# mLSTM and four experts on one core: w2's low halves made apart from chunk 4's scans, two outputs in two parts

## Chip, core and metric

The kernel runs on one core of one Trainium2 chip. The metric is device time in microseconds (us), lower is better. Times of the runs are medians; views of the profile come from one profiled execution.

## What is computed

An mLSTM layer (2 batches, 8 heads, 768 steps, head width 40) feeds a mixture of 4 experts (model width 320, hidden width 1024). All arrays are float32.

```python
# mLSTM, per time step t
m_new = max(f[t] + m, i[t])
C = exp(f[t] + m - m_new) * C + exp(i[t] - m_new) * outer(v[t], k[t])
n = exp(f[t] + m - m_new) * n + exp(i[t] - m_new) * k[t]
y[t] = sigmoid(o[t]) * (C @ q[t]) / max(|n . q[t]|, 1)
# experts on x = y, 1536 rows of 320
p = domain_probs / (domain_probs.sum(-1) + 1e-9)
out = sum over e of p[:, e] * (relu(x @ w1[e]) @ w2[e])
```

## The kernel before

The 1536 rows are cut into 12 chunks of 128 (`NCH`), 6 per batch. Every engine works through its instructions in the order in which the program issues them; nothing reorders them, so the order of the calls is the schedule. SyncE (SP) issues every transfer.

**A chunk n** needs: `decay(n)` (VectorE, two scans of 128x512 that build the decay matrix dd; for chunks 0 to 3 the factors fb come from TensorE and lie in PSUM, from chunk 4 on they come by a transfer of 512 KB, `load_f`, and lie in SBUF), `scores(n)` (TensorE), `weigh(n)` (VectorE, scores times dd), `values(n)` and `keys(n)` (GpSimd; `keys` needs dd), `inter(n)` (TensorE, then eight ScalarE copies into yb), `intra(n)` (TensorE), `norm(n)` (VectorE, six operations that end in xr), `state(n)` (TensorE, then two VectorE additions into the next state cs), `carry(n)` (GpSimd, the decayed state cd), `turn(n)` (three TensorE transposes of xr, then ScalarE copies into the high part of xst) and `turn_lo(n)` (VectorE, the low part).

**PSUM.** The results of `inter`, `intra`, `state` and `turn` (y1, y0, st, px) take turns in the pool `ps_y`, which has two buffers. So st takes the buffer of y1, px that of y0, and the next y1 and y0 those of st and px.

**The experts** use split numbers: each weight is a high part (float32r, made by a ScalarE copy, `split_hi`) and a low part (the difference, made by a subtraction, `split_lo`). `split_w2(f, 2)` does both for two of the eight hidden blocks f of w2; `quarter_hi(i)` and `quarter_lo(i)` do it for blocks 2i and 2i+1 of w1. Products are summed over three or more pairs of parts.

Expert 0 works on groups of 256 rows while the chunks go on. A group has four `hidden` steps (two blocks each: 16 matmuls on TensorE, relu on ScalarE for the high part of h, a VectorE operation for its low part) and two `output` steps (24 matmuls each: eight blocks times three pairs of h and w2 parts; then one ScalarE copy). For group 0 the list of an output is sorted so that the 16 matmuls with the high part of w2 come ahead of the 8 with its low part. `steps(k)` issues the next k steps; `SLOTS` says for each chunk how many stand after `decay`, after `carry`, and around `turn`. After chunk 11 come expert 0's last rows and experts 1 to 3, by 512 rows, on TensorE almost alone.

The raw w2 of expert 0 (`w2r`, 1,310,720 bytes) is requested at L603, behind `f_d` at L601. In the loop's turn n = 2, at L679 to L681, the four `split_w2` stand at its end, behind `carry(3)`. Turn n = 3 begins with `decay(4)` (L660), then `steps` with the hidden step of blocks 6 and 7 (L661).

Of the kernel before, what the change touches and what calls it, by code (L numbers as in the profile page):

```python
# [8 lines left out]
F32 = mybir.dt.float32  # L9
# [7 lines left out]
NE, DM, FF = 4, 320, 1024  # L17
NT = B * S
L = 128
# [6 lines left out]
NF = FF // L  # L26
HI, LO = 0, 1
# [9 lines left out]
NPE = 4  # L37

SLOTS = (
    (0, 1, 0), (1, 1, 1), (1, 1, 1), (1, 1, 0), (1, 1, 0),  # L40
    (1, 1, 0), (1, 1, 0), (1, 1, 0), (1, 1, 1), (0, 1, 1),
)
PAD = 56

# [5 lines left out]
def tile_mlstm_moe(ctx, tc, gt, qk, vk, ot, dp, w1, w2, out):  # L50
    ctx.enter_context(tc.manual_schedule())
    nc = tc.nc

    def pool(name, bufs, **kw):
        return ctx.enter_context(tc.tile_pool(name=name, bufs=bufs, **kw))
# [9 lines left out]
    ps_o = pool("ps_o", 2, space=PSUM)  # L65
# [22 lines left out]
    def new_weights(e):  # L88
        wp = wps[e % 2]
        w1s = wp.tile([L, KW, FF], F32R, tag="w1", name=f"w1s{e}")  # L90
        if e == 0:
            nc.gpsimd.memset(w1s[C:L, 5].bitcast(F32), 0.0)
        return w1s, wp.tile([L, 2, NF, DM], F32R, tag="w2", name=f"w2s{e}")

    def split_hi(hi, raw):
        nc.scalar.activation(hi, raw, AF.Copy)  # L96

    def split_lo(lo, hi, raw, eng):
        eng.tensor_sub(lo, raw, hi.bitcast(F32))  # L99
# [8 lines left out]
    def split_w2(ws, f0, n, raw, eng):  # L108
        f = slice(f0, f0 + n)
        split_hi(ws[:, HI, f], raw[:, f])  # L110
        split_lo(ws[:, LO, f], ws[:, HI, f], raw[:, f], eng)

    def load_w1e(e):
        raw1 = raws.tile([L, 3, FF], F32, tag="raw", name="raw1")
        nc.sync.dma_start(raw1, w1[e])
        return raw1
# [8 lines left out]
    class Expert:  # L125


        def __init__(self, e, t0, n, w1s, w2s):
            self.e, self.t0, self.n, self.w1s, self.w2s = e, t0, n, w1s, w2s
            self.nf, self.wide = W // n, n == W  # L130
            self.hs = []
            self.nh, self.no = NF // self.nf, n // L
            self.i = 0
            self.banks = []

        def step(self):
            i = self.i
            self.i += 1
            if i < self.nh:
                self.hidden(i * self.nf)  # L140
            elif i < self.nh + self.no:
                self.output(i - self.nh)
            return self.i < self.nh + self.no

        def hidden(self, f0):
            n, nf = self.n, self.nf
# [34 lines left out]
                    start=True, stop=False,  # L181
                )

        def output(self, t):
            e, ws = self.e, self.w2s
            po = ps_o.tile([L, DM], F32, tag="po", name="po")
            sl = slice(t * L, (t + 1) * L)
            ks = [(f, a, b) for f in range(NF) for a, b in ((HI, LO), (HI, HI), (LO, HI))]
            if e == 0 and self.t0 == 0:
                ks.sort(key=lambda k: k[2])  # L190
            for i, (f, a, b) in enumerate(ks):
                nc.tensor.matmul(  # L192
                    po, self.hs[f][a][:, sl], ws[:, b, f, :],
                    start=(i == 0), stop=(i == len(ks) - 1),
                )
            i = self.t0 // L + t
            if e == 0:
                nc.scalar.activation(acc[:, i, :], po, AF.Copy, scale=pw[:, i, 0:1])  # L198
            else:
                nc.vector.scalar_tensor_tensor(  # L200
                    out=acc[:, i, :], in0=po, scalar=pw[:, i, e:e + 1], in1=acc[:, i, :],
                    op0=ALU.mult, op1=ALU.add,
                )
            if e == NE - 1:
                nc.sync.dma_start(out[i * L:(i + 1) * L, :], acc[:, i, :])


    with ExitStack() as actx:
# [4 lines left out]
        w1s, w2s = new_weights(0)  # L213
        w1r = {}

        def quarter_hi(i):
            f, (ab, c) = slice(i * G, (i + 1) * G), w1r[i]
            split_hi(w1s[:, 0:2, f], ab)
            split_hi(w1s[:, 2, f], c)
# [138 lines left out]
        def load_qk(j, c=None):  # L358
            c = slice(0, 2) if c is None else slice(c, c + 1)
            nc.sync.dma_start(qks[j % 2][:, c], qk[j, :, c])  # L360

        def load_vk(j, c=None):
            if j not in vks:
                vks[j] = a2.tile([L, 2, 2, H, D], F32, tag="vk", name="vk")
            c = slice(0, 2) if c is None else slice(c, c + 1)
            nc.sync.dma_start(vks[j][:, c], vk[j, :, c])

        def load_o(j):
            nc.sync.dma_start(acc[:, 2 * j:2 * j + 2], ot[:, 2 * j:2 * j + 2])

        def gate_o(j):
            og = acc[:, 2 * j:2 * j + 2]
            nc.scalar.activation(og, og, AF.Sigmoid)
# [4 lines left out]
        def spread(n, pool, tag):  # L378

            b, c, k = n // NC, n % NC, 48 if n < 2 else L  # L380
            fbs[n] = [pool.tile([L, 4, L], F32, tag=tag, name="fb") for _ in range(2)]
            for h in range(H):
                nc.tensor.matmul(
                    fbs[n][h // 4][:, h % 4, :],
                    sel[0:k, b * H + h:b * H + h + 1].to_broadcast([k, L]),
                    fr[0:k, c * L:(c + 1) * L], start=True, stop=True,
                )

        def load_f(n):
            b, c = n // NC, n % NC  # L390
            fb = a0.tile([L, H, L], F32, tag=f"fb{n % 2}", name="fb")
            fbs[n] = fb[:, 0:4], fb[:, 4:8]
            nc.sync.dma_start(
                fb, f_d[b * H:(b + 1) * H, c * L:(c + 1) * L].unsqueeze(0).to_broadcast([L, H, L])
            )

        def decay(n):
            dds[n] = a1.tile([L, H, L], F32, tag=f"dd{n % 2}", name="dd")
            for i in range(2):
                nc.vector.tensor_tensor_scan(  # L400
                    out=dds[n][:, 4 * i:4 * i + 4].rearrange("p h t -> p (h t)"),
                    data0=fbs[n][i].rearrange("p h t -> p (h t)"),
                    data1=id4.rearrange("p h t -> p (h t)"),
                    initial=0.0, op0=ALU.mult, op1=ALU.add,
                )
# [8 lines left out]
        def keys(n):  # L414
            if n % NC < NC - 1:
                nc.gpsimd.tensor_mul(  # L416
                    kp[n % 2][:, :, 0:D], vks[n // 2][:, n % 2, 1],
                    dds[n][:, :, L - 1:L].to_broadcast([L, H, D]),
                )
# [37 lines left out]
        def carry(n):  # L457
            b, c = n // NC, n % NC
            if 0 < c < NC - 1:
                cd = cds[n] = a1.tile([104, NP, L], F32, tag="cd", name="cd")  # L460
                nc.gpsimd.tensor_mul(  # L461
                    cd, cs[c % 2][0:104],
                    bl[0:104, c, b * NP:(b + 1) * NP].unsqueeze(2).to_broadcast([104, NP, L]),
                )
# [63 lines left out]
        def steps(n):  # L528
            for _ in range(n):
                if not work[0].step():  # L530
                    work.pop(0)
# [70 lines left out]
        w2r = raws.tile([L, NF, DM], F32, tag="raw", name="w2r")  # L602
# [30 lines left out]
        gate_l(2, NC)  # L633
        spread(3, ps_o, "po")
        keys(2)
        carry(2)
        gctx.close()
        a0 = actx.enter_context(
# [4 lines left out]
        for n in range(2, NCH):  # L643
            j, cc = n // 2, n % 2
            k = SLOTS[n - 2]
            nxt = n + 1 < NCH
            if cc == 0 and j + 1 < NG:
                load_qk(j + 1)
                load_vk(j + 1)
            if NPE < n + 2 < NCH:  # L650
                load_f(n + 2)
            if cc == 0:
                if j > 1:
                    gate_o(j)
                if j + 1 < NG:
                    load_o(j + 1)
            if n == NCH - 2:
                raw1 = load_w1e(1)
            if nxt:
                decay(n + 1)  # L660
            steps(k[0])  # L661
            if n == 2:
                quarter_hi(2)
                quarter_lo(2)
            inter(n)
            intra(n)
            norm(n)
            if n == 2:
                quarter_hi(3)
                quarter_lo(3)  # L670
            if nxt:
                scores(n + 1)
            state(n)
            if nxt:
                values(n + 1)
                keys(n + 1)
                weigh(n + 1)
                carry(n + 1)
            if n == 2:  # L679
                for f in range(0, NF, 2):  # L680
                    split_w2(w2s, f, 2, w2r, nc.gpsimd)  # L681
            steps(k[1])
            if cc == 0:
                steps(k[2])
            turn(n)
            turn_lo(n)
            if cc == 1:
                steps(k[2])
# [112 lines left out]
```

## Time and profile before

| | us |
|---|---|
| median of 3 runs (411.93 to 412.13) | 411.93 |
| the profiled execution | 413.2 |
| span of its profile | 411.4 |
| TensorE busy in the span | 401.2 |
| VectorE, ScalarE, GpSimd busy | 181.6, 125.2, 85.2 |

In the rows further below, PE is TensorE (PEld its weight loads), DVE VectorE, ACT ScalarE, POOL GpSimd, SPq SyncE's queue of transfers. L192 is line 192: the matmuls of `output`; L157 those of `hidden`; L400 the scans; L96 and L99 the copies and subtractions that split weights. A number in brackets is time in which the engine sat idle before the row, with what ended it. PEclk is the granted clock of TensorE as a share of 2.4 GHz (0.50 is 1.2 GHz). Times count from the start of the span.

### The profile page before, as it was taken

How to read it: one execution, taken by the hardware profiler on the slowest of the kernel's cores; microseconds unless marked ns; L12 is line 12 of the kernel's file. 1: busy time of each engine (PE TensorE's matmuls, PEld its weight loads, DVE VectorE, ACT ScalarE, POOL GpSimd, SP SyncE). 2: the span in 40 equal slices, each digit the busy share in tenths (PEclk: the TensorE clock that was granted, in tenths of full speed). 3: DMA queues.
4: the chain of work that ended last, by engine and by line, in shares of the span. 5: the costliest groups of instructions: out<-in, count | busy, mean ns of one | idle time of the engine just before them, and what ended most of it. 6: DMA issues, size and time to landing. Idle time of an engine off the chain costs nothing.

```text
span 411.4 us, 7176 instructions
## 1 busy us (share of the span) xinstructions
PE 401.2 (98%) x3042; PEld 363.2 (88%) x3042; DVE 181.6 (44%) x319; ACT 125.2 (30%) x298; POOL 85.2 (21%) x98
## 2 busy tenths in 40 slices
PE   9899699999999999999999999999999999999996
PEld 5699599999988898998988988989989889899896
DVE  8989958697962303314214234133142251231321
ACT  5676133352433533205213032033030140220210
POOL 6869401223112630003410010016100010000000
PEclk9999699999999999999999999999999999999999
DMA  7997514576000213000300004002000000001001
GB/s 212 309 287 203 162 53 106 177 200 237 2 2 2 77 52 118 35 2 0 129 0 2 0 2 153 2 2 90 39 0 2 0 2 32 33 0 49 17 18 48
DMA packets 15080, 29.34 MB, mean 71 GB/s; under 512 B 1000, under 2 KB 10728, under 8 KB 13736
## 3 DMA queue, kind: packets, MB, share of 16 engines
q1 hardware_dynamic: 15048, 28.88, 22.8%
q8 instruction: 24, 0.39, 0.4%
q14 instruction: 8, 0.07, 0.1%
HBM read 26.86 MB, written 2.02 MB: 70 GB/s over the span
## 4 chain that ended last, share of the span: by engine, by line
PE 89%; DVE 8%; issue 2%; ACT 0%; DVEq 0%
PE po L192 41%; PE ph L157 37%; DVE dd L400 3%; PE ph L179 3%; PE s L427 2%; PE y L489 2%; PE y L474 1%; DVE pm L433 1%; PE px L516 1%; PE st L445 1%; DVE h L167 1%; DVE mb L267 0%; DVE cs L455 0%; DVE xr L506 0%; DVE gat L292 0%
## 5 line engine op out<-in xcount | busy, mean ns | idle before, releaser
L192 PE MATMUL po<-w2s,h 128*128 128x320 f32 x1152 | 175.3, 312 | 3.8 <-DVE h L167 3.8
L192 PEld LDWEIGHTS po<-w2s,h 128*128 128x128 f32 x1152 | 172.1, 190 | 5.1 <-DVE h L167 4.1
L157 PE MATMUL ph<-xst,w1s 128*128 128x512 f32 (+1 forms) x816 | 164.1, 359 | 0.0
L157 PEld LDWEIGHTS ph<-xst,w1s 128*128 128x128 f32 x816 | 135.8, 189 | 24.2 <-issue 2.4
L166 ACT ACTIVATE h<-ph 128x512 fp32r<-128x512 f32 x96 | 57.5, 598 | 196.6 <-PE ph L157 196.6
L167 DVE SCALAR_TENSOR_TENSOR h<-ph,h 128x512 fp32r<-128x512 f32 x96 | 66.2, 689 | 103.6 <-ACT h L166 103.1
L200 DVE SCALAR_TENSOR_TENSOR acc<-po,pw,acc 128x320 f32<-128x320 f32 x36 | 19.8, 551 | 99.9 <-PE po L192 99.9
L99 POOL TENSOR_TENSOR w1s<-raw,w1s 128x512 fp32r<-128x512 f32 (+1 forms) x24 | 23.5, 1029 | 74.5 <-ACT w1s L96 67.4
L400 DVE TENSOR_TENSOR_SCAN dd<-fb,id 128x512 f32<-128x512 f32 x24 | 34.0, 1458 | 0.3
L99 POOL TENSOR_TENSOR w2s<-raw,w2s 128x640 fp32r<-128x640 f32 x6 | 9.4, 1574 | 98.2 <-ACT w2s L96 98.2
L198 ACT ACTIVATE acc<-po,pw 128x320 f32<-128x320 f32 x12 | 6.3, 527 | 43.4 <-PE po L192 43.4
L481 ACT ACTIVATE yb<-y,ibT 128x41 f32<-128x41 f32 x80 | 15.9, 311 | 3.4 <-PE y L474 3.4
L433 DVE TENSOR_TENSOR pm<-s,dd 128x512 f32<-128x512 f32 x24 | 15.5, 686 | 0.5
L427 PE MATMUL s<-qk 64*128 64x128 f32 (+1 forms) x192 | 14.1, 285 | 0.0
L489 PE MATMUL y<-vp,pm 128*64 128x41 f32 x384 | 13.2, 228 | 0.9 <-DVE xst L524 0.9
L96 ACT ACTIVATE w2s<-raw 128x640 fp32r<-128x640 f32 x12 | 8.8, 734 | 16.4 <-DMA raw<-in_w 16.4
L489 PEld LDWEIGHTS y<-vp,pm 128*64 128x64 f32 x384 | 12.5, 138 | 1.3 <-POOL w1s L699 1.1
L427 PEld LDWEIGHTS s<-qk 64*128 64x128 f32 (+1 forms) x192 | 11.8, 187 | 1.4 <-DVE pm L433 0.8
L416 POOL TENSOR_TENSOR kp<-vk,dd 128x320 f32<-128x320 f32 x10 | 7.4, 735 | 26.9 <-DVE dd L400 26.9
L461 POOL TENSOR_TENSOR cd<-cs,bl 104x512 f32<-104x512 f32 x8 | 9.1, 1139 | 15.0 <-DVE cs L455 11.6
L411 POOL TENSOR_TENSOR vp<-vk,ibT 128x320 f32<-128x320 f32 x12 | 9.6, 800 | 12.1 <-issue 9.4
L179 PE MATMUL ph<-xd,w1s 64*128 64x512 f32 x40 | 12.0, 419 | 0.0
(91 smaller groups left out, 210.1 us busy)
## 6 DMA issues: line engine op xcount, KB each, us to landing
raw<-in_w SPq DMA_DIRECT2D x3, 1536.0 KB, 6.6
fb<-f_d SPq DMA_DIRECT2D x8, 512.0 KB, 8.3
raw<-in_w SPq DMA_DIRECT2D x3, 1280.0 KB
qk<-in_qk SPq DMA_DIRECT2D x4, 832.0 KB
vk<-in_vk SPq DMA_DIRECT2D x4, 640.0 KB, 9.1
acc<-in_ot SPq DMA_DIRECT2D x6, 320.0 KB, 9.3
out<-acc SPq DMA_DIRECT2D x12, 160.0 KB, 1.8
qk<-in_qk SPq DMA_DIRECT2D x4, 416.0 KB
```

The costliest lines, as they stand in the source:

```text
L99: eng.tensor_sub(lo, raw, hi.bitcast(F32))
L157: nc.tensor.matmul(ph[:, i, :], self.w1s[:, wi, f * L:(f + 1) * L], xst[:, xi, self.t0:self.t0 + n], start=(k == 0 and not self.wide), sto ...
L166: nc.scalar.activation(hh, ph, AF.Relu)
L167: nc.vector.scalar_tensor_tensor(out=hl, in0=ph, scalar=0.0, in1=hh.bitcast(F32), op0=ALU.max, op1=ALU.subtract)
L179: nc.tensor.matmul(self.banks[f][:, 0, :], self.w1s[r, 5, f * L:(f + 1) * L], x, start=True, stop=False,)
L192: nc.tensor.matmul(po, self.hs[f][a][:, sl], ws[:, b, f, :], start=(i == 0), stop=(i == len(ks) - 1),)
L200: nc.vector.scalar_tensor_tensor(out=acc[:, i, :], in0=po, scalar=pw[:, i, e:e + 1], in1=acc[:, i, :], op0=ALU.mult, op1=ALU.add,)
L400: nc.vector.tensor_tensor_scan(out=dds[n][:, 4 * i:4 * i + 4].rearrange("p h t -> p (h t)"), data0=fbs[n][i].rearrange("p h t -> p (h t)") ...
L427: nc.tensor.matmul(ss[n][r][:, p, :], kg[q, p], qg[q, p], start=True, stop=True)
L433: nc.vector.tensor_mul(pm[:, r], ss[n][r], dd[:, r])
L481: nc.scalar.activation(yb[:, h], y1[:, h, 0:D + 1], AF.Copy, scale=ibT[:, c, i:i + 1])
L489: nc.tensor.matmul(y[t, h, 0:D + 1], pms[n][:, h, t], vvs[n][:, h, 0:D + 1], start=True, stop=True,)
```

## The change

Four things are moved or cut.

1. The four `split_w2` no longer stand at the end of turn 2. Blocks 0 and 1 are split ahead of the loop, between `keys(2)` and `carry(2)`. In turn 3 blocks 2 and 3 stand behind the hidden step and ahead of `decay(4)`; blocks 4 to 7 stand behind `decay(4)` and `keys(4)`, ahead of `inter(3)`.
2. In turn 3 the hidden step of blocks 6 and 7 stands ahead of `decay(4)`, and `keys(4)` is called right behind it.
3. The two outputs of group 0 are cut into a part with the high weights (16 matmuls) and one with the low weights (8). The order is: high part of the first, high part of the second, low part of the first, low part of the second. Group 0 so has 8 steps in place of 6, and turn 3 takes two steps more (one behind `carry(4)`, three behind `turn(3)`).
4. In `SLOTS`, turn 10 takes one step less and turn 11 one more: the last hidden step of group 3 moves from ahead of `turn(10)` to ahead of `inter(11)`.

```diff
-    (0, 1, 0), (1, 1, 1), (1, 1, 1), (1, 1, 0), (1, 1, 0),
-    (1, 1, 0), (1, 1, 0), (1, 1, 0), (1, 1, 1), (0, 1, 1),
+    (0, 1, 0), (1, 1, 3), (1, 1, 1), (1, 1, 0), (1, 1, 0),
+    (1, 1, 0), (1, 1, 0), (1, 1, 0), (1, 1, 0), (1, 1, 1),
...
+            todo = [(self.hidden, (f,)) for f in range(0, NF, self.nf)]
+            ts = range(n // L)
+            if e == 0 and t0 == 0:
+                todo += [(self.output, (t, p)) for p in (HI, LO) for t in ts]
+            else:
+                todo += [(self.output, (t,)) for t in ts]
...
-        def output(self, t):
+        def output(self, t, part=None):
...
-            if e == 0 and self.t0 == 0:
-                ks.sort(key=lambda k: k[2])
+            first, last = part != LO, part != HI
+            if first:
+                self.pos[t] = ps_o.tile([L, DM], F32, tag="po", name="po")
+            if part is not None:
+                ks = [k for k in ks if k[2] == part]
+            po = self.pos[t]
...
+                    start=(first and i == 0), stop=(last and i == len(ks) - 1),
                 )
+            if not last:
+                return
...
         keys(2)
+        split_w2(w2s, 0, 2, w2r, nc.gpsimd)
         carry(2)
...
-            if nxt:
+            if n == 3:
+                steps(k[0])
+                split_w2(w2s, 2, 2, w2r, nc.gpsimd)
                 decay(n + 1)
-            steps(k[0])
+                keys(n + 1)
+                for f in (4, 6):
+                    split_w2(w2s, f, 2, w2r, nc.gpsimd)
+            else:
+                if nxt:
+                    decay(n + 1)
+                steps(k[0])
...
                 values(n + 1)
-                keys(n + 1)
+                if n != 3:
+                    keys(n + 1)
                 weigh(n + 1)
                 carry(n + 1)
-            if n == 2:
-                for f in range(0, NF, 2):
-                    split_w2(w2s, f, 2, w2r, nc.gpsimd)
             steps(k[1])
```

## Rows read from the trace of the kernel before

**Rows 1.** Chain that ended last, in order of time: start, length, what.

```profile
37.88 5.06 issue
...
97.16 0.33 PE px L516 x3
97.49 3.52 PE po L192 x24
```

**Rows 2.** Timeline of TensorE: start, length, line, count, [idle before].

```profile
31.63 2.17 PE L157 MATMUL ph<-xst,w1s 128*128 128x256 f32 x16
...
35.96 0.94 PE L474 MATMUL y<-cs,qk 104*64 104x105 f32 x16
...
38.84 0.51 PE L445 MATMUL st<-vp,kp 128*40 128x41 f32 x16
39.27 2.17 PE L192 MATMUL po<-w2s,h 128*128 128x320 f32 x13
45.24 3.30 PE L192 MATMUL po<-w2s,h 128*128 128x320 f32 x11 [3.79 <-DVE h L167]
...
53.46 2.08 PE L157 MATMUL ph<-xst,w1s 128*128 128x256 f32 x16
```

**Rows 3.** Windows: stretch, busy us of PE, PEld, DVE, ACT, POOL, PEclk, DMA share, GB/s.

```profile
19.00:20.00 1.00, 0.19 (x1) 0.00 (x0) 0.90 (x4) 0.99 (x3) 1.00 (x2) 1.00 1.03 388
...
50.00:51.00 1.00, 1.00 (x5) 1.00 (x5) 0.94 (x3) 0.00 (x0) 0.00 (x0) 0.50 0.00 0
```

**Rows 4.** Timeline of VectorE.

```profile
28.81 2.33 DVE L400 TENSOR_TENSOR_SCAN dd<-fb,id 128x512 f32<-128x512 f32 x2
...
36.27 6.74 DVE L400 TENSOR_TENSOR_SCAN dd<-fb,id 128x512 f32<-128x512 f32 x1
...
45.11 0.49 DVE L502 TENSOR_TENSOR y<-y,yb 128x328 f32<-128x328 f32 x1
...
46.69 0.49 DVE L509 TENSOR_TENSOR xr<-xr,y 128x320 f32<-128x320 f32 x1
```

**Rows 5.** Timeline of GpSimd.

```profile
28.25 1.04 POOL L461 TENSOR_TENSOR cd<-cs,bl 104x512 f32<-104x512 f32 x1 [1.04 <-ACT bl L339]
29.25 1.27 POOL L99 TENSOR_TENSOR w1s<-wa,w1s 128x512 fp32r<-128x512 f32 x1
...
35.83 6.06 POOL L99 TENSOR_TENSOR w2s<-w2r,w2s 128x640 fp32r<-128x640 f32 x4
41.85 1.67 POOL L411 TENSOR_TENSOR vp<-vk,ibT 128x320 f32<-128x320 f32 x1
44.68 0.74 POOL L416 TENSOR_TENSOR kp<-vk,dd 128x320 f32<-128x320 f32 x1 [1.16 <-DVE dd L400]
```

**Rows 6.** Timeline of ScalarE.

```profile
27.91 0.19 ACT L339 ACTIVATE bl<-pit 128x32 f32<-128x32 f32 x1
...
31.66 2.66 ACT L96 ACTIVATE w2s<-w2r 128x640 fp32r<-128x640 f32 x4
...
36.13 0.60 ACT L166 ACTIVATE h<-ph 128x512 fp32r<-128x512 f32 x1 [0.93 <-PE ph L157]
36.95 1.59 ACT L481 ACTIVATE yb<-y,ibT 128x41 f32<-128x41 f32 x8 [0.23 <-PE y L474]
```

**Rows 7.** Turns 10 and 11: timelines of TensorE and VectorE.

```profile
111.89 4.10 PE L157 MATMUL ph<-xst,w1s 128*128 128x256 f32 x32
...
118.13 1.13 PE L489 MATMUL y<-vp,pm 128*64 128x41 f32 x32 [0.93 <-DVE xst L524]
...
113.21 0.49 DVE L509 TENSOR_TENSOR xr<-xr,y 128x320 f32<-128x320 f32 x1
```

**Rows 8.** The loop's rest, and the transfers: windows, and SyncE's timeline.

```profile
53.50:126.80 73.30, 72.37 (x939) 69.20 (x938) 53.07 (x111) 28.81 (x103) 14.60 (x18) 1.00 0.37 109
...
22.00:27.00 5.00, 5.00 (x55) 4.95 (x56) 4.64 (x8) 3.45 (x6) 3.19 (x4) 1.00 0.94 307
...
22.18 0.38 SPq L393 DMA_DIRECT2D fb<-f_d  x1
```

More of the change, by code (lines that the diff above doesn't have):

```diff
@@ L130, in __init__ @@
             self.nf, self.wide = W // n, n == W
[L131 to L134, printed above, removed]
-        def step(self):
[L137 to L143, printed above, removed]
+            self.hs, self.banks, self.pos = [], [], {}
+            todo = [(self.hidden, (f,)) for f in range(0, NF, self.nf)]
[4 more added lines that the diff above has]
+                todo += [(self.output, (t,)) for t in ts]
+            self.todo = todo
+        def step(self):
+            f, args = self.todo.pop(0)
+            f(*args)
+            return bool(self.todo)
         def hidden(self, f0):
@@ L182, in corners @@
                 )
-        def output(self, t):
+        def output(self, t, part=None):
             e, ws = self.e, self.w2s
-            po = ps_o.tile([L, DM], F32, tag="po", name="po")
             sl = slice(t * L, (t + 1) * L)
             ks = [(f, a, b) for f in range(NF) for a, b in ((HI, LO), (HI, HI), (LO, HI))]
-            if e == 0 and self.t0 == 0:
-                ks.sort(key=lambda k: k[2])
+            first, last = part != LO, part != HI
[4 more added lines that the diff above has]
+            po = self.pos[t]
             for i, (f, a, b) in enumerate(ks):
@@ L193, in output @@
                     po, self.hs[f][a][:, sl], ws[:, b, f, :],
-                    start=(i == 0), stop=(i == len(ks) - 1),
+                    start=(first and i == 0), stop=(last and i == len(ks) - 1),
                 )
+            if not last:
+                return
             i = self.t0 // L + t
```

## Prediction

> **What bounds the kernel now.** I read the engines' busy times first: TensorE is busy for 401.2 of the 411.4 us of the span, so time is to be had only where it idles or runs slowly. In the windows of the loop's rest and behind it there is nearly none of that: from 53.5 to 126.8 TensorE is busy for 72.4 of 73.3 us at full clock [rows 8]. The chain of waits then says where else to look. It runs through TensorE nearly everywhere, but at 37.88 it has a stretch of 5.06 us in which nothing is released, inside a scan [rows 1]. The timelines show why. GpSimd makes the four low parts of w2 back to back from 35.83 to 41.89 [rows 5]. VectorE begins the first scan of chunk 4 at 36.27, and that scan takes 6.74 us [rows 4], where two scans of the same shape together take 2.33 [rows 4]. It ends 1.1 us after the last subtraction, so it waited for all four. Behind it on VectorE stands the low part of h for blocks 6 and 7, and TensorE, 13 matmuls into the first output, waits for that until 45.24 [rows 2]. By then its clock has fallen: 0.50, the 1.2 GHz level, still at 50 to 51 [rows 3].
>
> What the stretch costs: from the first output's start at 39.27 to the next group's first hidden step at 53.46 it took 14.19 us [rows 2]. Its work is 48 matmuls and three transposes; at full clock 24 such matmuls take 3.52 us, so 0.147 each, and the transposes 0.33 [rows 1]: 7.05 + 0.33 = 7.4. So **6.8 us** can be had here. Of it the clock cost 2.8: from 45.24 to 53.46 are 8.22 us for 35 matmuls and the transposes, which are 5.46 at full clock. The rest is idle time. A second place is turn 11, where TensorE waits 0.93 us for turn_lo(10) to release the buffer of px [rows 7].
>
> **The change part by part.**
>
> Hidden step ahead of the scans. The low part of h no longer stands behind the scans, and that wait of TensorE goes. The matmuls and VectorE operations are the same in number. Next in line are the four things below.
>
> Blocks 0 and 1 split ahead of the loop. On ScalarE the copy follows the one that ends at 28.10 [rows 6] and takes 2.66 / 4 = 0.66 [rows 6], to 28.8. The subtraction takes 6.06 / 4 = 1.51 on GpSimd [rows 5], to 30.3, and carry(2) stands behind it, 1.0 from its start to the next one's [rows 5], to 31.3. Behind that stand quarter_lo(2) and (3), values, keys and carry of chunk 3: GpSimd has no gap there that could take it in. The first low part of w1's quarter 2, 1.27 long [rows 5], so ends at 32.6 in place of 30.5. The hidden step of blocks 4 and 5 begins at 31.63 [rows 2] and needs it for its second matmul. It waits about **0.9 us**, and so does all that TensorE does behind it; the later low parts then come in time. If GpSimd should lag less the cost is nothing, so 0 to 0.9; I take 0.9, for each term has its row. That subtraction runs beside the scans of chunk 3, which read PSUM and one SBUF operand; beside w1's subtractions these same scans took 2.33 and the subtraction 1.27 [rows 4, 5], so neither holds the other up.
>
> Three copies on ScalarE ahead of inter(3)'s. inter(3) moves from 35.96 to 36.86 on TensorE; its chunk work up to the state's matmuls takes 38.84 - 35.96 = 2.88 [rows 2], to 39.74. On ScalarE h of blocks 6 and 7 moves from 36.13 [rows 6] to 37.03 and ends at 37.63. Before, the copies of inter(3) into yb followed at once, 1.59 in all [rows 6]. Now three weight copies, 2.0, stand between, and yb is done at 37.63 + 2.0 + 1.59 = 41.2, less 0.1 because successive records overlap. The state's result takes the PSUM buffer of inter's result, and so waits for yb: TensorE idles from 39.74 to 41.1, **1.4 us**. This is the wait that replaces the old one.
>
> Scans and blocks 2 and 3. VectorE comes free for the scans when the low part of h is done, at about 38.3. At 38.3 the copy of blocks 2 and 3 is done too, and GpSimd starts its subtraction. One of them waits for the other. In the trace before, values(4) on GpSimd, asked for at 41.85, took 1.67 [rows 5], and came between the two scans. (Between the four subtractions the scan did not get its turn; here only one stands in GpSimd's queue, because keys(4) behind it waits for the scans, so 1.51 is the most.) In either order the scans end at 38.3 + 2.33 + 1.51 = 42.15; only if both scans go first do they end at 40.6. norm(3) takes 46.69 + 0.49 - 45.11 = 2.07 [rows 4], so xr(3) is there at 44.2. TensorE, with the state from 41.1 (0.43 to its end [rows 2]) and the 16 high matmuls of the first output (2.35), comes to the transposes at 43.9: it waits **0.3 us**, or nothing.
>
> The Trainium skill (SBUF — State Buffer, section "Who interferes with whom") says that a VectorE instruction with two SBUF inputs and a GpSimd instruction that reads SBUF exclude each other for the whole instruction of whichever starts first, and that a VectorE instruction with at most one SBUF input stays out of it. By that rule the first scan would have come in behind the first subtraction, at 37.4, and the second behind the next, and TensorE would have idled for about 0.7 us at full clock: an estimate by which this stretch would have 0.7 us to give and not 6.8. The trace agrees with the exclusion and not with the turn: 6.74 us [rows 4], so the row decides.
>
> Outputs in parts. The number of matmuls is the same, and both results have a buffer of their own; cost nothing. The low parts need the subtractions of blocks 4 to 7: behind keys(4), 0.74 [rows 5], and two of 1.51 they are done at 42.15 + 0.74 + 3.02 = 45.9. TensorE comes to them at 44.2 + 0.33 + 2.35 = 46.9. The cover is 1.0 us; what is later than that is paid in full. SP's queue: no transfer is moved; chunk 6's `load_f` waits for the scans and so goes earlier.
>
> Sum of this stretch: 44.2 + 0.33 + 32 matmuls (4.7) = 49.25 in place of 53.46, so **4.2 us**; or 6.8 - 0.9 - 1.4 - 0.3.
>
> Turns 10 and 11. The hidden step taken out of turn 10 is half of 4.10 [rows 7]. TensorE then comes to turn(10) at 111.89 + 2.0 = 113.9, and xr(10) is done at 113.70 [rows 7]: no wait, by 0.2. The step stands ahead of inter(11) and covers the turn's copies and turn_lo, which now come 2.0 earlier by TensorE, bounded by VectorE's queue to some 0.9 earlier. That covers the wait: **0.9 us**, with 0 as the other end.
>
> Sum: 4.2 + 0.9 = 5.1. In the profiled execution 413.2 - 5.1 = 408.1; the median of the runs is 1.27 below that execution, so 411.93 - 5.1 = **406.8**.
>
> **The rivals.**
>
> *Both scans pass ahead of the subtraction.* Then xr(3) waits for yb alone (41.1 + 2.07 = 43.2) and the 0.3 go: 406.5. If GpSimd's lag were also nothing, 405.6. For it: the instructions start within 0.1 us of each other. Against it: values(4) came between the scans. 0.12.
>
> *The clock falls.* TensorE idles 0.9, 1.4 and 0.3 within 13 us. If the clock fell as before it would cost those 2.8 us again: 409.6. Against: it idled for most of 19 to 20 and kept its 1.00 [rows 3], and 0.93 in turn 11 left it there too [rows 7, 8]. 0.10.
>
> *w2's raw values come late (slower).* The copy of blocks 0 and 1 now stands at 28.1 on ScalarE, ahead of all of quarter 2. The trace shows the values used first at 31.66 [rows 6]; they were there then, not when they came. `f_d`, requested just ahead of them, had landed by 22.18, where `load_f`, which reads it, was issued; 1.31 MB at 307 GB/s [rows 8] are 4.3 us, so 26.5, 1.6 us ahead of need, if the queue serves in order. Beyond 28.1 each us costs one. From about 31.0 TensorE's idle time reaches the old 3.8, and the clock with it: 406.8 + 2.9 + 2.8 = 412.5, and up to 413.2 at 31.66. 0.05.
>
> *The subtractions of blocks 4 to 7 hold up norm(3).* They run from 42.9 to 45.9, beside it. If its operations waited as the scan did, xr(3) would be 3.0 later: 409.8. Against: of two operands each reads at least one from PSUM, as the scans of chunk 3 do. (The skill's rule above says that such operations stay out; by it this rival has no chance.) 0.04.
>
> *The loop takes the gain back*, because VectorE or a transfer bounds chunks 5 to 11: then only turn 11's 0.9 is left, 411.0. Against: TensorE has no gap there [rows 8], and transfers are issued by buffers that come free with it. 0.06.
>
> **How the numbers follow.** The forecast has 0.63. Forecast, passing scans and clock hold 0.85, so the range goes from 405.4 to 409.7. A difference under 0.2% (0.8 us) can't be told from none. Faster: 0.63 + 0.12 + 0.10 + 0.04 = 0.89; same: 0.06; slower: 0.05.
>
> **What would show it.** In the profile of the changed kernel: the first scan of chunk 4 within 3 us, at most one w2 subtraction beside the two; a wait of the hidden step of blocks 4 and 5 for GpSimd near 31.8; one of the state's matmuls for ScalarE's yb, 1.4 us; a short one of the transposes for VectorE; PEclk 1.00 throughout; the second group's first hidden step near 49.3; no wait for turn_lo(10). A copy of w2 waiting on a transfer near 28 would make it wrong, and so would a clock of 0.50 after 40.

## The result

The changed kernel takes 407.65 us (median of 4 runs, 407.62 to 407.68), the kernel before 412.03 (4 runs, 411.93 to 412.37): a ratio of 0.9892, with a 95% interval of 0.9875 to 0.9909. That is 4.4 us less, where 5.1 were forecast (406.8). The profiled execution of the changed kernel took 407.64 us, its span is 405.8.

TensorE's timeline in the stretch that mattered, of the changed kernel (start, length, line, count, [idle before and what ended it]); it answers to [rows 2]. Line numbers have moved: L480 is inter, L433 scores, L451 state, L196 output.

```profile
31.62 0.39 PE L157 MATMUL ph<-xst,w1s 128*128 128x256 f32 x1
32.62 2.06 PE L157 MATMUL ph<-xst,w1s 128*128 128x256 f32 x15 [0.61 <-POOL w1s L99]
...
36.85 0.94 PE L480 MATMUL y<-cs,qk 104*64 104x105 f32 x16
...
38.63 1.16 PE L433 MATMUL s<-qk 64*128 64x128 f32 x16
41.07 0.51 PE L451 MATMUL st<-vp,kp 128*40 128x41 f32 x16 [1.27 <-POOL w2s L99]
41.51 2.61 PE L196 MATMUL po<-w2s,h 128*128 128x320 f32 x16
44.00 0.52 PE L522 MATMUL px<-ident,xr 128*128 128x128 f32 x3
44.27 4.94 PE L196 MATMUL po<-w2s,h 128*128 128x320 f32 x32
49.05 2.07 PE L157 MATMUL ph<-xst,w1s 128*128 128x256 f32 x16
```

The reader sees two new waits, 0.61 for a low part of w1 and 1.27 ahead of the state, and no third. The first of them sets inter(3) back by 0.89 in all, to 36.85 (35.96 in [rows 2]). The transposes at 44.00 follow the 16 high matmuls at once. The next group's first hidden step starts at 49.05; it stood at 53.46 in the profile of before, and 49.25 was forecast.

GpSimd's timeline of the changed kernel beside those of VectorE and ScalarE (L406 scans, L515 the last step of norm, L96 copies of w2, L487 copies into yb):

```profile
28.79 1.55 POOL L99 TENSOR_TENSOR w2s<-w2r,w2s 128x640 fp32r<-128x640 f32 x1 [1.59 <-ACT w2s L96]
30.30 1.04 POOL L467 TENSOR_TENSOR cd<-cs,bl 104x512 f32<-104x512 f32 x1
31.30 1.27 POOL L99 TENSOR_TENSOR w1s<-wa,w1s 128x512 fp32r<-128x512 f32 x1
...
38.32 2.48 POOL L99 TENSOR_TENSOR w2s<-w2r,w2s 128x640 fp32r<-128x640 f32 x1 [0.74 <-ACT w2s L96]
...
42.71 3.10 POOL L99 TENSOR_TENSOR w2s<-w2r,w2s 128x640 fp32r<-128x640 f32 x2
```

```profile
38.25 3.62 DVE L406 TENSOR_TENSOR_SCAN dd<-fb,id 128x512 f32<-128x512 f32 x2
41.80 0.48 DVE L508 TENSOR_TENSOR y<-y,yb 128x328 f32<-128x328 f32 x1
...
43.37 0.49 DVE L515 TENSOR_TENSOR xr<-xr,y 128x320 f32<-128x320 f32 x1
```

```profile
37.51 1.98 ACT L96 ACTIVATE w2s<-w2r 128x640 fp32r<-128x640 f32 x3
39.39 1.58 ACT L487 ACTIVATE yb<-y,ibT 128x41 f32<-128x41 f32 x8
```

The two scans of chunk 4 take 3.62 us together (1.22 and 2.49), against 6.74 for the first alone in [rows 4]. One subtraction meets them and takes 2.48 in place of 1.55: it starts 0.06 behind the first scan and ends 1.33 behind that scan's end, and the second scan ends 1.08 behind it. So it waits for the first scan, and the second scan waits for it.

Windows of the changed kernel (stretch, busy us of PE, PEld, DVE, ACT, POOL, PEclk, DMA share, GB/s), of the stretch and of the loop's rest, which answer to [rows 3, 8]; then TensorE in turn 11, to [rows 7]:

```profile
39.20:49.30 10.10, 8.82 (x82) 8.50 (x79) 9.86 (x16) 2.99 (x14) 8.68 (x7) 1.00 0.83 227
53.50:126.80 73.30, 73.30 (x894) 69.42 (x891) 53.39 (x112) 27.68 (x97) 14.60 (x18) 1.00 0.35 102
```

```profile
111.86 0.94 PE L480 MATMUL y<-cs,qk 104*64 104x105 f32 x16
112.63 1.08 PE L495 MATMUL y<-vp,pm 128*64 128x41 f32 x32
```

The clock keeps 1.00 in both stretches, and the mean over the whole execution is 0.999. In turn 11 intra follows inter after 0.77 us, without a wait.

### The profile page after: what moved, and what is told of

The parts are those of the page before. It is cut to its first block, busy times and chain, and to the rows that moved or that the text cites. A ratio compares the mean times of both kernels' runs of the same rounds, so it can differ in the third digit from the quotient of the medians.

```text
span 405.8 us, 7174 instructions
## 1 busy us (share of the span) xinstructions
PE 397.9 (98%) x3042; PEld 360.5 (89%) x3042; DVE 178.4 (44%) x319; ACT 125.1 (31%) x298; POOL 86.2 (21%) x98
## 4 chain that ended last, share of the span: by engine, by line
PE 92%; DVE 5%; issue 1%; POOL 1%; ACT 0%; DVEq 0%; POOLq 0%
PE po L196 42%; PE ph L157 39%; PE ph L179 3%; PE s L433 2%; PE y L495 2%; PE y L480 2%; DVE dd L406 2%; PE px L522 1%; PE st L451 1%; DVE pm L439 1%; DVE mb L273 0%; POOL w1s L99 0%; DVE gat L298 0%; POOL cd L467 0%; DVE cs L564 0%
## 5 line engine op out<-in xcount | busy, mean ns | idle before, releaser
L196 PE MATMUL po<-w2s,h 128*128 128x320 f32 x1152 | 172.6, 310 | 0.0
L196 PEld LDWEIGHTS po<-w2s,h 128*128 128x128 f32 x1152 | 169.8, 188 | 1.0
L406 DVE TENSOR_TENSOR_SCAN dd<-fb,id 128x512 f32<-128x512 f32 x24 | 30.7, 1320 | 0.2
L487 ACT ACTIVATE yb<-y,ibT 128x41 f32<-128x41 f32 x80 | 15.9, 313 | 2.9 <-PE y L480 2.9
L96 ACT ACTIVATE w2s<-raw 128x640 fp32r<-128x640 f32 x12 | 8.8, 734 | 17.4 <-DMA raw<-in_w 17.4
L433 PE MATMUL s<-qk 64*128 64x128 f32 (+1 forms) x192 | 14.1, 285 | 0.0
L433 PEld LDWEIGHTS s<-qk 64*128 64x128 f32 (+1 forms) x192 | 11.8, 187 | 1.4 <-DVE dd L406 0.8
L179 PE MATMUL ph<-xst,w1s 64*128 64x512 f32 x40 | 12.0, 418 | 0.0
```

The lines of the kernel that those rows point to most:

```text
L179: nc.tensor.matmul(self.banks[f][:, 0, :], self.w1s[r, 5, f * L:(f + 1) * L], x, start=True, stop=False,)
L196: nc.tensor.matmul(po, self.hs[f][a][:, sl], ws[:, b, f, :], start=(first and i == 0), stop=(last and i == len(ks) - 1),)
L406: nc.vector.tensor_tensor_scan(out=dds[n][:, 4 * i:4 * i + 4].rearrange("p h t -> p (h t)"), data0=fbs[n][i].rearrange("p h t -> p (h t)") ...
L433: nc.tensor.matmul(ss[n][r][:, p, :], kg[q, p], qg[q, p], start=True, stop=True)
L487: nc.scalar.activation(yb[:, h], y1[:, h, 0:D + 1], AF.Copy, scale=ibT[:, c, i:i + 1])
```

## The experiments

There are ten runs. Ratios are to runs of the kernel before on the same chip beside them (median 412.3); the 407.65 of the changed kernel, with which some are compared, is from the result above, where the kernel before stood at 412.03. In the traces the start of the next group's first hidden step, 49.05 in the changed kernel, moves by the same amounts within 0.1 us. No run puts the hidden step of blocks 6 and 7 back behind the scans by itself, so what its new place is worth beside the separation is not shown.

**Turn 11 alone.** The kernel before with one line of `SLOTS` changed.

```diff
-    (1, 1, 0), (1, 1, 0), (1, 1, 0), (1, 1, 1), (0, 1, 1),
+    (1, 1, 0), (1, 1, 0), (1, 1, 0), (1, 1, 0), (1, 1, 1),
```

> The kernel before with the last part of the change alone: the last hidden step of group 3 moves from ahead of turn(10) to ahead of inter(11). Theory (the step covers the copies of turn 10, so the 0.93 us wait of TensorE for turn_lo(10) goes): 0.9 to 1.1 us below the kernel before, and no wait of intra(11) in the trace. Rival (turn(10) comes 2 us earlier than xr(10), and the wait moves there): no difference, and a wait of the transposes for VectorE near 114.

Measured: 411.19 us, ratio 0.9978 (0.9967 to 0.9989), so 0.9 us below the kernel before (0.5 to 1.4). Its TensorE timeline has intra at 0.77 behind inter, with no wait:

```profile
116.48 0.94 PE L474 MATMUL y<-cs,qk 104*64 104x105 f32 x16
117.25 1.09 PE L489 MATMUL y<-vp,pm 128*64 128x41 f32 x32
```

The theory holds; the transposes of turn 10 did not wait either.

**Separation undone.** The changed kernel with all four splits back at the end of turn 2.

```diff
-        split_w2(w2s, 0, 2, w2r, nc.gpsimd)
         carry(2)
...
                 steps(k[0])
-                split_w2(w2s, 2, 2, w2r, nc.gpsimd)
                 decay(n + 1)
                 keys(n + 1)
-                for f in (4, 6):
-                    split_w2(w2s, f, 2, w2r, nc.gpsimd)
...
+            if n == 2:
+                for f in range(0, NF, 2):
+                    split_w2(w2s, f, 2, w2r, nc.gpsimd)
             steps(k[1])
```

> The changed kernel with the separation undone: all four w2 splits stand again at the end of turn 2, ahead of chunk 4's scans; the hidden step ahead of the scans, the outputs in parts and turn 11 stay. Theory (the separation carries the gain): the subtractions run from 35.8 to 41.9, the first scan waits for all four and takes about 4.6 us from 37.4, xr(3) comes near 46.3, TensorE stands from 41.6 to 46.3 ahead of the transposes and its clock falls; the next group's first hidden step near 54.1, the time about 0.5 us below the kernel before (turn 11's 1.1 less 0.65), near 411.5. Rival (the order of hidden step and scans carries it): near the changed kernel, 407 to 408.

Measured: 411.92 us, ratio 0.9982 (0.9971 to 0.9992). VectorE and TensorE:

```profile
37.45 6.76 DVE L406 TENSOR_TENSOR_SCAN dd<-fb,id 128x512 f32<-128x512 f32 x2
```

```profile
46.34 0.88 PE L522 MATMUL px<-ident,xr 128*128 128x128 f32 x3 [4.37 <-DVE xr L515]
46.87 7.29 PE L196 MATMUL po<-w2s,h 128*128 128x320 f32 x32
53.99 2.08 PE L157 MATMUL ph<-xst,w1s 128*128 128x256 f32 x16
```

The wait for the low part of h is gone, and a longer one for xr(3) stands in its place. The first scan alone took 5.65 us; the 4.6 that were expected are its wait. The 32 matmuls behind the wait take 7.29 us, against 4.94 in the changed kernel: PEclk is 0.50 from 46 to 52. Without the separation, hidden step and parts give nothing here: the ratio is no lower than that of turn 11 alone.

**Outputs whole.** The changed kernel with the two outputs of group 0 in one part each.

```diff
-    (0, 1, 0), (1, 1, 3), (1, 1, 1), (1, 1, 0), (1, 1, 0),
+    (0, 1, 0), (1, 1, 1), (1, 1, 1), (1, 1, 0), (1, 1, 0),
...
-                todo += [(self.output, (t, p)) for p in (HI, LO) for t in ts]
+                todo += [(self.output, (t,)) for t in ts]
...
-            if part is not None:
-                ks = [k for k in ks if k[2] == part]
+            if e == 0 and self.t0 == 0:
+                ks.sort(key=lambda k: k[2])
```

> The changed kernel with the two outputs of group 0 whole again (24 matmuls each, low weights last). Theory: the first output reaches the low weights of blocks 4 to 7 at 44.4 and waits for the last subtraction until 45.8, 1.1 to 1.4 us; the transposes wait no more; so 0.9 us above the changed kernel, 408.6. Rival (the parts do nothing because the transposes' wait for VectorE or another wait takes that place): the same as the changed kernel within 0.2.

Measured: 408.75 us, ratio 0.9909 (0.9894 to 0.9923), 1.1 above the changed kernel. TensorE waits for the last subtraction, and the next group's first hidden step starts at 50.11 in place of 49.05:

```profile
45.86 0.56 PE L196 MATMUL po<-w2s,h 128*128 128x320 f32 x2 [0.84 <-POOL w2s L99]
```

**The two new waits, one by one and together.** First, blocks 0 and 1 are split at the end of turn 2, behind carry(3).

```diff
-        split_w2(w2s, 0, 2, w2r, nc.gpsimd)
         carry(2)
...
+            if n == 2:
+                split_w2(w2s, 0, 2, w2r, nc.gpsimd)
             steps(k[1])
```

> The changed kernel with one thing undone: blocks 0 and 1 of w2 are split at the end of turn 2, behind carry(3), not ahead of carry(2). Theory (that subtraction delays GpSimd's quarter of w1 and with it TensorE by 0.9 us): no wait of the hidden step of blocks 4 and 5, the wait of the state's matmuls for yb stays at about 1.3 us, the next group's first hidden step near 48.15, the time 0.9 us below the changed kernel, 406.75. Rival (the delay is eaten by the wait for yb or for xr(3) that follows): within 0.3 us of the changed kernel.

Measured: 406.81 us, ratio 0.9860 (0.9845 to 0.9875), 0.84 below the changed kernel. The hidden step of blocks 4 and 5 no longer waits; the state does, and the next group's first hidden step is at 48.17:

```profile
40.19 0.51 PE L451 MATMUL st<-vp,kp 128*40 128x41 f32 x16 [1.28 <-POOL w2s L99]
...
48.17 2.07 PE L157 MATMUL ph<-xst,w1s 128*128 128x256 f32 x16
```

Second, only the ScalarE copies of blocks 2 to 7 move to the end of turn 2.

```diff
+        def w2_lo(f):
+            split_lo(w2s[:, LO, f:f + 2], w2s[:, HI, f:f + 2], w2r[:, f:f + 2], nc.gpsimd)
...
-                split_w2(w2s, 2, 2, w2r, nc.gpsimd)
+                w2_lo(2)
                 decay(n + 1)
                 keys(n + 1)
                 for f in (4, 6):
-                    split_w2(w2s, f, 2, w2r, nc.gpsimd)
+                    w2_lo(f)
...
+            if n == 2:
+                for f in (2, 4, 6):
+                    split_hi(w2s[:, HI, f:f + 2], w2r[:, f:f + 2])
             steps(k[1])
```

> The changed kernel with the ScalarE copies of blocks 2 to 7 moved to the end of turn 2; all subtractions stay where they are. Theory: the wait of the state's matmuls for yb, 1.3 us, goes, but the transposes of turn 3 then wait about 0.9 us for xr(3), because the subtraction of blocks 2 and 3 begins at once behind carry(3) and holds VectorE's first scan until about 39.1; so only 0.4 us below the changed kernel, 407.2. Rival (the wait for yb is the whole price): 1.3 us below it, 406.3.

Measured: 407.12 us, ratio 0.9867 (0.9852 to 0.9882), 0.53 below the changed kernel.

```profile
39.74 0.51 PE L451 MATMUL st<-vp,kp 128*40 128x41 f32 x16
...
43.41 0.52 PE L522 MATMUL px<-ident,xr 128*128 128x128 f32 x3 [0.62 <-DVE xr L515]
```

The state's wait is gone with the copies. In the changed kernel the profile had named GpSimd's subtraction as what ended it; the state's matmuls read nothing that this writes, and yb was done at 39.39 + 1.58 = 40.97, 0.1 ahead of them. The wait for xr(3) takes over, as the theory says, so the whole price of 1.27 is not to be had by this alone.

Third, both at once, and the subtraction of blocks 2 and 3 behind keys(4) as well (`w2_lo` as in the run above).

```diff
-        split_w2(w2s, 0, 2, w2r, nc.gpsimd)
         carry(2)
...
                 steps(k[0])
-                split_w2(w2s, 2, 2, w2r, nc.gpsimd)
                 decay(n + 1)
                 keys(n + 1)
-                for f in (4, 6):
-                    split_w2(w2s, f, 2, w2r, nc.gpsimd)
+                for f in (2, 4, 6):
+                    w2_lo(f)
...
+            if n == 2:
+                for f in range(0, NF, 2):
+                    split_hi(w2s[:, HI, f:f + 2], w2r[:, f:f + 2])
+                w2_lo(0)
             steps(k[1])
```

> A version beyond the change: the four ScalarE copies of w2 stand at the end of turn 2 as in the kernel before, the subtraction of blocks 0 and 1 right behind carry(3), the other three behind keys(4); all else as in the changed kernel. Theory (in the changed kernel TensorE pays 0.9 us for the subtraction ahead of carry(2) and 1.3 us for the three copies ahead of yb): both waits go, the next group's first hidden step comes near 46.8 in place of 49.05, and the time is 2.2 us below the changed kernel, 405.4. Rival (VectorE or GpSimd ends last in that stretch anyway, so the low parts or the scans take the place of these waits): within 0.5 us of the changed kernel.

Measured: 405.55 us, ratio 0.9831 (0.9817 to 0.9846) to the kernel before, 2.1 below the changed kernel. Chunk 4's scans meet no subtraction (chunk 5's, from 44.25, take 3.60 us beside the end of the last one), and TensorE waits for nothing in the stretch:

```profile
37.37 2.33 DVE L406 TENSOR_TENSOR_SCAN dd<-fb,id 128x512 f32<-128x512 f32 x2
```

```profile
38.84 0.51 PE L451 MATMUL st<-vp,kp 128*40 128x41 f32 x16
39.27 2.61 PE L196 MATMUL po<-w2s,h 128*128 128x320 f32 x16
41.82 0.52 PE L522 MATMUL px<-ident,xr 128*128 128x128 f32 x3
42.09 4.94 PE L196 MATMUL po<-w2s,h 128*128 128x320 f32 x32
46.87 2.07 PE L157 MATMUL ph<-xst,w1s 128*128 128x256 f32 x16
```

This version is faster than both kernels.

**What the scan waits for.** First, two of the four splits are left ahead of the scans in the kernel before, two go behind keys(4).

```diff
             if nxt:
                 decay(n + 1)
+            if n == 3:
+                keys(n + 1)
+                for f in (4, 6):
+                    split_w2(w2s, f, 2, w2r, nc.gpsimd)
             steps(k[0])
...
-                keys(n + 1)
+                if n != 3:
+                    keys(n + 1)
...
             if n == 2:
-                for f in range(0, NF, 2):
+                for f in (0, 2):
                     split_w2(w2s, f, 2, w2r, nc.gpsimd)
```

> The kernel before with two of the four splits (blocks 4 to 7) behind keys(4), the other two at the end of turn 2 as before. Theory (a scan waits for the whole run of subtractions ahead of it): the first scan waits for two, and takes about 3.7 us from 36.3; the second ends near 41.2, the low part of h is done near 41.9 and TensorE's clock stays up; about 4 us below the kernel before, near 408. Rival (the length of the run does not matter, the scan is slowed by something else): the first scan takes 6 us or more again.

Measured: 409.82 us, ratio 0.9927 (0.9900 to 0.9955). The two subtractions ran from 35.83 to 38.87. The first scan, TensorE's waits and a window behind them:

```profile
36.27 3.68 DVE L400 TENSOR_TENSOR_SCAN dd<-fb,id 128x512 f32<-128x512 f32 x1
```

```profile
41.70 1.28 PE L192 MATMUL po<-w2s,h 128*128 128x320 f32 x7 [0.27 <-DVE h L167]
43.51 0.56 PE L192 MATMUL po<-w2s,h 128*128 128x320 f32 x2 [0.52 <-POOL w2s L99]
45.01 0.89 PE L192 MATMUL po<-w2s,h 128*128 128x320 f32 x2 [0.95 <-POOL w2s L99]
```

```profile
45.00:46.00 1.00, 0.99 (x4) 0.95 (x5) 0.54 (x1) 0.06 (x1) 1.00 (x2) 0.53 1.14 318
```

The first scan took 3.68 us, where the theory has 3.7: the delay goes with the number of subtractions. The time was a miss by nearly 2 us: TensorE waits 0.27, 0.52 and 0.95 us for single parts, and behind the last of these the clock falls in this execution (410.58 us, mean clock 0.996); in two of the four it did not (409.05, mean clock 1.00).

Second, a small memset stands behind each subtraction of the kernel before.

```diff
+        gap = const.tile([L, 32], F32, name="gap")
...
                     split_w2(w2s, f, 2, w2r, nc.gpsimd)
+                    nc.gpsimd.memset(gap, 0.0)
```

> The kernel before with one thing added: a small GpSimd memset (128x32) behind each of the four subtractions. Theory (back to back, the next subtraction takes the port before the waiting scan can; an instruction that reads no SBUF in between lets the scan in): the first scan ends near 38.7 in place of 43.0, the second near 41, TensorE waits for the low part of h less than 1 us, its clock keeps 1.00, and the time is 3 us or more below the kernel before, near 408. Rival (the scan waits until GpSimd has no such subtraction left): the first scan takes 6.7 us again, the time is that of the kernel before.

Measured: 414.68 us, ratio 1.0050 (1.0032 to 1.0067). The rival was right that the scan waits for all four:

```profile
36.83 7.62 DVE L400 TENSOR_TENSOR_SCAN dd<-fb,id 128x512 f32<-128x512 f32 x1
```

```profile
36.39 1.54 POOL L99 TENSOR_TENSOR w2s<-w2r,w2s 128x640 fp32r<-128x640 f32 x1
37.88 0.11 POOL L683 MEMSET gap<- 128x32 f32 x1
37.96 1.52 POOL L99 TENSOR_TENSOR w2s<-w2r,w2s 128x640 fp32r<-128x640 f32 x1
...
42.65 0.71 POOL L411 TENSOR_TENSOR vp<-vk,ibT 128x320 f32<-128x320 f32 x1
```

A memset between two subtractions did not let the scan in. Here values(4), the last line above, went ahead of the scan too, which makes it 7.62 us and not 6.74. The time is above the kernel before for other reasons as well: the scan starts 0.56 us later than in [rows 4], and in the rest of this execution six of the ten long hidden stretches of 512 rows take 13.2 us where all ten take 12.9 to 13.0 before. The new tile shifts what lies behind it in memory; that this is the cause is not shown.

**The kernel before again.** Twice, unchanged.

> The kernel before, unchanged, profiled again. Theory (the time that the low clock takes in the stretch from 45 on differs from execution to execution, by about 1.2 us, and the profiled execution of before at 413.2 us is of the longer kind): either a span near 410.4 with the clock back at 1.00 by about 49, and the next group's first hidden step near 52.3, or one near 411.4 with the clock back at 51. Rival (the 1.2 us are elsewhere, at the start or the end of the execution): the first hidden step near 53.4 whatever the time.

> The kernel before, unchanged, profiled once more, as the run before this: the theory expects the start of the next group's first hidden step to move with the time, 52.3 at 412.2 us and 53.4 at 413.2; the rival expects it to stay.

Measured: 412.26 and 412.04 us. The next group's first hidden step, in the first execution and then in the second, and a window of the first:

```profile
52.55 2.07 PE L157 MATMUL ph<-xst,w1s 128*128 128x256 f32 x16
```

```profile
52.35 2.08 PE L157 MATMUL ph<-xst,w1s 128*128 128x256 f32 x16
```

```profile
49.00:50.00 1.00, 1.00 (x8) 1.00 (x7) 0.59 (x2) 0.54 (x2) 0.80 (x2) 0.88 0.00 0
```

The step moves with the time, as the theory says: 53.46 at 413.2 us, 52.55 at 412.26, 52.35 at 412.04. The idle time ahead is nearly the same (3.97 and 3.79, against 3.79). The clock was back at 1.00 by 50 in these two, and only after 51 in the profile that the prediction was worked from.

## Why the prediction was right, and where it was off

*The stretch before.* Idle time and low clock were the two things to be had, and both went. The size of the clock's part was the mis-sized term. 2.8 us was right for the profiled execution at 413.2 us. In the two at 412.0 to 412.3 the low clock cost less: 45.23 to 52.35 are 7.12 us for work of 5.46, so 1.7. Of the 23 runs of the kernel before beside the first experiments, 17 took 411.9 to 412.4 us at a mean granted clock of 0.996 and 6 took 412.9 to 413.5 at 0.992; the profile that the prediction was worked from (413.2, 0.992) is like the 6, the median like the 17. So carrying the profile's sum over to the median by subtracting it took 1.1 us too much. The other way, the gains forecast from the terms below were together 0.4 too small (4.2 against 4.4 in the stretch, 0.9 against 1.1 in turn 11), which leaves the 0.7 between 5.1 and 4.4.

*The low part of w1, 0.9.* inter(3) started at 36.85; 36.86 was forecast. Taken away alone it gave 0.84.

*The wait for yb, 1.4.* 1.27 measured. Removed alone it gives 0.53: TensorE then comes to the transposes 0.62 ahead of xr(3), which stands only 0.6 earlier than in the changed kernel (43.27 against 43.86).

*Scans and subtraction, 42.15.* The scans ended at 41.87, 0.3 sooner. Most of that is the handover: the subtraction ended 1.33 behind the first scan's end, where 1.51 was added; why is not shown. So the transposes' wait of 0.3 did not come: xr(3) was done at 43.86, and TensorE came to them at 44.00.

*Outputs in parts: nothing, with 1.0 of cover.* The last subtraction ended at 45.81 (45.9 forecast), and TensorE came to the low weights at about 46.6, so the cover was 0.8. Without the parts 1.1 us are paid.

*Turns 10 and 11, 0.9.* 0.9 (0.5 to 1.4) when timed alone; by the traces 1.1, because intra stood 1.87 behind inter before and 0.77 after.

Put together, as the executions near the median have it: 52.35 - 49.05 = 3.3 in the stretch, and 1.1 in turn 11, so 4.4.

*The rivals.* The subtraction came between the two scans, so they did not both pass ahead of it. The loop did not take the gain back: the lead of 4.41 us at the next group's first hidden step is 4.38 at turn 10's (111.89 - 107.51). norm(3) was not held up by blocks 4 to 7: 41.80 to 43.86 are 2.06 us, the last half of it beside subtractions that began at 42.71. The raw w2 was there at 28: ScalarE's copy started at 27.98 behind its predecessor. The clock kept 1.00, but the run with two splits ahead of the scans shows that this rival was not idle: behind three waits of under 1 us each the clock fell in the profiled execution, and by the mean clocks in two of the four.

## What to carry to other kernels

Where GpSimd runs a row of long SBUF subtractions, look for VectorE operations with both inputs in SBUF that become ready behind the first of them: here their delay was the rest of the row, and it landed on whatever stood behind them on VectorE. When such a row is moved, count what moves with it: here the copies that feed it, on ScalarE, and the older work queued behind it, on GpSimd, cost 2.1 us, which a better place won back. And where a stretch runs at the low clock, take its cost from several executions before it goes into a sum.

## What was not expected of the hardware

A scan that was waiting did not get in between two of these subtractions in any trace here: with two in a row the first scan took 3.68 us, with four 6.74, and with a memset between each it did not get in either. In the run with blocks 0 and 1 behind carry(3), the scan came free just as a subtraction ended (37.37), 0.06 us ahead of the next one's start, and there it went first. Between the last subtraction and values(4) it went either way: in [rows 5] values took 1.67 and so waited for the scan, and in one of the two later executions of the same kernel it took 0.71 and went ahead (first scan 7.41). The Trainium skill (SBUF — State Buffer, section "Who interferes with whom") has the exclusion, and that the one that starts first keeps the port for the whole instruction; the 2.48 us of the changed kernel's subtraction agree with that. Who is next does not follow the order of starts: the scan of [rows 4], started at 36.27, let pass three subtractions that started behind it. What decides it the runs leave open.

The time at the low clock differed between executions of the same kernel with nearly the same idle time ahead of it. In [rows 3] PEclk is still 0.50 at 50 to 51; in the two later executions it is 0.88 and 0.72 at 49 to 50 and 1.00 from 50 on. In the first it had also fallen sooner: 0.64 at 44 to 45, while the other two still show 0.91 and 1.00 at 45 to 46.
